# Order on the tensor engine in a KV-cache decode kernel: value sums ahead of a new load's first transposes, and both transposes of the 40-key load ahead of the value sums

## Chip, cores and metric

One core of a Trainium2 chip; later batches of runs were on other chips, so medians are compared within the same rounds. The metric is the device time of one execution in microseconds, from the first to the last instruction and the launch around it; the profile's own span is 1.7 to 2.1 us shorter.

## The reference

One token through a layer-norm, attention over a cache of 32 heads with 32768 keys of 192 numbers each, an output projection, and a small ReLU block. Cut to what matters:

```python
H, Sk, Dh = 32, 32768, 192                      # bf16
scores = einsum("bhqd,bhkd->bhqk", q, k_cache) * Dh ** -0.5
p = softmax(scores); o = einsum("bhqk,bhkd->bhqd", p, v_cache)
h = x + o.reshape(1, 1, H * Dh) @ wo;  out = h + relu(layernorm(h) @ w1) @ w2
```

K and V together are 805 MB, each byte used once.

## The kernel before

Each head is read in four K loads and four V loads of 3072 KB (128 partitions x 64 keys). One load is worked on in two chunks of 32 keys; the last head's last load is cut into 40, 16 and 8 keys per partition, so that little is left to do after the last byte. In each chunk DVE does the dot products of some keys; PE does the rest: it transposes K tiles (`transposes`), ACT copies them out of four PSUM buffers, PE multiplies them with q (`scores_pe`), ACT takes the exponentials (`ep` for PE's keys, `ed` for DVE's), and PE sums the values (`values`). Instructions stand in each engine's queue in the order of the program, and on PE matmuls came out in that order: in the profile before, the last head's value sums of chunk 3, whose inputs were complete at 1884.6 us, start at 1890.16, behind transposes that waited for their load until 1886.77.

```python
def transposes(g, h, c):                        # cut
    if off == 0: g.wait("at", "k", h, ld)       # first chunk of a load: its K has landed
    for k, (b0, nb) in enumerate(tiles(jp)):    # up to 4 tiles, 4 PSUM buffers
        g.wait("cp", *tile_before(h, t))        # ACT has emptied this buffer
        ...

def values(g, h, c):                            # cut
    g.wait("ep", h, c); g.wait("ed", h, c)      # probabilities of this chunk
    ...                                         # 16 matmuls

def pe_head(g, h, turn=None):
    for c in range(NC):                         # NC = 8 chunks
        transposes(g, h, c)
        if c > 0:
            values(g, h, c - 1)
        elif h > 0:
            values(g, h - 1, NC - 1)
            den_mm(g, h - 1)
        scores_pe(g, h, c)
        ...                                     # projection, next head's q

# the SP queue, in the order of its issues (cut):
load(K of load n)
g.wait("PV", hp, 2 * lp + 1)                    # value sums of load n-2's second chunk
load(V of load n)                               # two V buffers
```

So a V buffer is released by the value sums of an odd chunk, and these stood behind the first transposes of the next K load, which wait for that load to land.

The softmax here doesn't subtract the row's maximum and nothing guards it: scores larger than these inputs give would overflow.

## Time and profile before

| | before |
|---|---|
| time, median of the first 3 runs | 1926.88 us (1926.21 to 1927.18) |
| bytes read | 825 MB, 427 to 435 GB/s in every slice of the span but the first (408) and the last (321) |
| PE / DVE / ACT busy | 81% / 80% / 50% |
| PE's wait for a K load at its first transposes | 341.8 us, 127 times |

In the profile's lines, `POOLq L301` is GpSimd's relay, which tells PE that a load has landed.

The page's chain of work that ended last, before (share of the span by engine), says where time is set:

```profile
DMA 76%; PE 22%; SPq 1%; issue 0%; ACT 0%; POOLq 0%; DVE 0%
```

Walked back from the end, almost every step leads to the landing of a K load. In the timeline's lines, the columns are start, duration, engine, line, operation, tiles and count; a bracket gives the idle time before it and what ended it. One more line of the timeline before will be needed, the first transposes of the 40-key load:

```profile
1899.69 1.18 PE L338 MATMUL tp<-ident_f,kt 128*128 128x128 f32 x9
```

The 40-key load had landed at 1898.5.

### The profile page before, as it was taken

What the parts mean: (1) busy time and instruction counts of PE and PEld (TensorE: products, weight loads), DVE (VectorE), ACT (ScalarE), POOL (GpSimd) and SP (SyncE); (2) the same over time, 40 slices, a digit from 0 to 9 for tenths busy, and PEclk for the clock granted to TensorE, in tenths of its full rate; (3) what the DMA queues carried; (4) which work ended last, traced back from release to release, by engine and by line L of the source; (5) the groups of instructions that cost most, each with busy time, mean ns of one, the idle gap of its engine ahead of it and who ended that gap; (6) DMA issues with size and microseconds to landing.
All of it is one profiled execution on the core that took longest, in us unless ns stands there. A gap on an engine that the chain in (4) does not pass through costs nothing.

```text
span 1925.6 us, 36082 instructions
## 1 busy us (share of the span) xinstructions
PE 1563.4 (81%) x15899; PEld 1074.8 (56%) x15899; DVE 1546.3 (80%) x670; ACT 970.6 (50%) x2031; POOL 0.7 (0%) x6
## 2 busy tenths in 40 slices
PE   5887888787887888788788878888778888888788
PEld 4555555555555555555555555555555555555555
DVE  5888888787887888887788878888778887888786
ACT  4554555454554554555454554545445454545554
POOL 0000000000000000000000000000000000000000
PEclk8889888888989898888888888888888888898888
DMA  9999999999999999999999999999999999999997
GB/s 408 430 432 433 433 432 432 433 433 431 433 430 433 433 433 433 433 432 427 434 433 433 433 431 433 430 435 432 430 431 431 435 432 433 431 431 429 431 432 321
DMA packets 44799, 825.31 MB, mean 429 GB/s; under 512 B 4580, under 2 KB 6116, under 8 KB 12132
## 3 DMA queue, kind: packets, MB, share of 16 engines
q1 hardware_dynamic: 44762, 824.99, 99.8%
q8 instruction: 12, 0.20, 0.0%
q14 instruction: 15, 0.12, 0.0%
q10 hardware_dynamic: 10, 0.00, 0.0%
HBM read 824.97 MB, written 0.00 MB: 428 GB/s over the span
## 4 chain that ended last, share of the span: by engine, by line
DMA 76%; PE 22%; SPq 1%; issue 0%; ACT 0%; POOLq 0%; DVE 0%
DMA kt<-in_A_k_cache_dram 76%; PE o_ps L319 11%; PE tp L338 10%; SPq L221 1%; PE mm L319 1%; PE sp L319 0%; PE attT L319 0%; ACT kT L533 0%; POOLq L301 0%; DVE o_pair L631 0%; ACT pB L539 0%; PE mm L522 0%; ACT h1T L595 0%; DVE y_row L699 0%; DVE h_col L681 0%
## 5 line engine op out<-in xcount | busy, mean ns | idle before, releaser
L617 DVE TENSOR_TENSOR pr<-kt,qb 128x2304 f32<-128x2304 bf16 (+2 forms) x257 | 755.8, 2941 | 298.9 <-DMA kt<-in_A_k_cache_dram 282.6
L533 ACT COPY kT<-tp 128x1024 bf16<-128x1024 bf16 (+1 forms) x899 | 818.9, 992 | 342.2 <-PE tp L338 340.2
L338 PE MATMUL tp<-ident_f,kt 128*128 128x128 f32 x3459 | 571.7, 332 | 341.8 <-POOLq L301 341.8
L620 DVE TENSOR_REDUCE sc<-pr 128x12 f32<-128x2304 f32 (+2 forms) x257 | 755.3, 2939 | 8.9
L338 PEld LDWEIGHTS tp<-ident_f,kt 128*128 128x128 f32 x3459 | 498.1, 173 | 358.7 <-POOLq L301 357.5
L319 PE MATMUL o_ps<-vt,pB 128*2 128x384 bf16 x2286 | 470.9, 357 | 3.5 <-POOLq L301 3.4
L319 PE MATMUL o_ps<-vt,pA 128*2 128x384 bf16 x1778 | 331.0, 326 | 0.0
L319 PEld LDWEIGHTS o_ps<-vt,pB 128*2 128x2 bf16 x2286 | 184.1, 89 | 239.8 <-issue 87.6
L539 ACT ACTIVATE pB<-sp 128x20 bf16<-128x20 f32 (+2 forms) x258 | 47.9, 186 | 503.1 <-PE sp L319 503.1
L319 PEld LDWEIGHTS sp<-qm,kT 128*128 128x128 bf16 x6918 | 193.2, 97 | 77.7 <-issue 67.5
L319 PEld LDWEIGHTS o_ps<-vt,pA 128*2 128x2 bf16 x1778 | 151.0, 85 | 144.7 <-issue 8.1
L319 PE MATMUL sp<-qm,kT 128*128 128x2 bf16 x6918 | 212.0, 164 | 3.0 <-ACT kT L533 2.1
L548 ACT ACTIVATE pA<-sc 128x12 bf16<-128x12 f32 (+2 forms) x257 | 53.4, 208 | 89.0 <-DVEq L64 88.3
L539 ACT ACTIVATION_READ_ACCUMULATOR pB<-sp 128x1 f32 x258 | 50.2, 195 | 0.0
L548 ACT ACTIVATION_READ_ACCUMULATOR pA<-sc 128x1 f32 x257 | 48.7, 190 | 0.0
L625 DVE TENSOR_REDUCE rec<-mm 128x1 f32<-128x20 f32 x32 | 5.7, 179 | 51.6 <-PE mm L319 51.1
L319 PE MATMUL mm<-wq_s,xn_ln 128*1 (+1 forms) x160 | 18.7, 248 | 3.6 <-POOLq L301 3.6
L631 DVE TENSOR_SCALAR o_pair<-o_ps,rec 2x384 bf16<-2x384 f32 x32 | 19.4, 605 | 2.8 <-PE o_ps L319 1.7
L319 PE MATMUL attT<-oT,wo_s 128*128 128x1 bf16 x465 | 15.9, 163 | 0.3 <-DVE oT L638 0.3
L319 PEld LDWEIGHTS mm<-dsums,ones_mat 128*128 128x128 f32 x64 | 9.5, 188 | 10.7 <-issue 9.3
L319 PE MATMUL mm<-ones_row,row_e 1*128 1x1 bf16 x384 | 14.0, 159 | 0.0
L319 PEld LDWEIGHTS attT<-oT,wo_s 128*128 128x128 bf16 x465 | 13.8, 95 | 0.3 <-DVE oT L638 0.3
(69 smaller groups left out, 129.1 us busy)
## 6 DMA issues: line engine op xcount, KB each, us to landing
kt<-in_A_k_cache_dram SPq DMA_DIRECT2D x127, 3072.0 KB, 22.5
vt<-in_A_v_cache_dram SPq DMA_DIRECT2D x127, 3072.0 KB, 15.5
wq_s<-in_A_wq_dram SPq DMA_DIRECT2D x4, 1920.0 KB, 21.9
wo_s<-in_A_wo_dram SPq DMA_DIRECT2D x16, 480.0 KB, 16.3
kt<-in_A_k_cache_dram SPq DMA_DIRECT2D x1, 1920.0 KB, 19.7
kt<-in_A_v_cache_dram SPq DMA_DIRECT2D x2, 960.0 KB, 24.3
kt<-in_B_w_dram SPq DMA_DIRECT2D x1, 1920.0 KB, 18.3
wq_s<-in_B_w_dram SPq DMA_DIRECT2D x1, 960.0 KB, 20.3
```

The source lines that it names most:

```text
L221: g.do(lambda: nc.sync.dma_start(out=dst, in_=src), sem, label, by=16)
L319: return lambda: pe.matmul(o, lhsT=w, rhs=r, **kw)
L338: calls.append(lambda b=b, o=o: pe.transpose(out=dst[:, b, :], in_=src[:, o:o + 2 * P].bitcast(f32), identity=ident_f[:]))
L533: g.do(lambda: act.copy(out=kT[c % 2][:, b0:b0 + nb, :], in_=src[:, 0:nb, :].bitcast(bf16)), "act_pe", ("cp", h, c, k))
L539: g.do(lambda: act.activation(out=pB[c % 4][:, 0:jp], in_=sp[:, 0:jp], func=F.Exp, scale=SCALE, accum_out=dsums[:, 2 * c + 1:2 * c + 2]), ...
L548: g.do(lambda: act.activation(out=pA[c % 4][:, 0:jd], in_=sc[c % NC][:, 0:jd], func=F.Exp, scale=SCALE, accum_out=dsums[:, 2 * c:2 * c + 1 ...
L617: g.chain(lambda: dve.tensor_tensor(out=pr[:, 0:j1 - j0, :], in0=src[:, (off + j0) * Dh:(off + j1) * Dh].rearrange("p (j d) -> p j d", d=D ...
L620: g.chain(lambda: dve.reduce_sum(out=sc[c % NC][:, j0:j1], in_=pr[:, 0:j1 - j0, :], axis=X), "dve")
L625: g.chain(lambda: dve.reduce_sum(out=rec[:, 0:1], in_=mm[:, 0:2 * NCM], axis=X), "dve")
L631: g.do(lambda: dve.tensor_scalar_mul(out=o_pair[:, :, h % 2, :], in0=o_ps[0:2, 0:2 * Dh].rearrange("q (i d) -> q i d", i=2), scalar1=rec[0 ...
```

## The change

The intent: PE should not stand before a load that has not landed while value sums are ready; V buffers would come free earlier. At the end, the transposes of both halves of the 40-key load go first, so that ACT gets their copies sooner.

```diff
+    def pe_chunk(g, h, c):
+        if c % 2 == 1:
+            transposes(g, h, c)
+        if c > 0:
+            values(g, h, c - 1)
+        elif h > 0:
+            values(g, h - 1, NC - 1)
+            den_mm(g, h - 1)
+        if c % 2 == 0:
+            transposes(g, h, c)
+        scores_pe(g, h, c)
     def pe_head(g, h, turn=None):
         for c in range(NC):
-            transposes(g, h, c)
-            ...                     # values, den_mm, scores as above
+            pe_chunk(g, h, c)
     # the last head: pe_chunk for chunks 0 to 5 in the same way (cut), then, E0 = 6:
         transposes(g, h, E0)
+        transposes(g, h, E0 + 1)
         values(g, h, E0 - 1)
-        for c in range(E0 + 1, NCM):
-            transposes(g, h, c)
-            scores_pe(g, h, c - 1)
-            if c > E0 + 1:
-                values(g, h, c - 2)
+        scores_pe(g, h, E0)
+        transposes(g, h, E0 + 2)
+        scores_pe(g, h, E0 + 1)
+        values(g, h, E0)
+        ...                         # E0 + 3 in the same way as before
```

More of the change, by code (lines that the diff above doesn't have):

```diff
@@ L442, in q_spread @@
         pe_group(g, calls, ("qs", h), "pe_act")
+    def pe_chunk(g, h, c):
[9 more added lines that the diff above has]
+        scores_pe(g, h, c)
     def pe_head(g, h, turn=None):
         for c in range(NC):
-            transposes(g, h, c)
-            if c > 0:
-                values(g, h, c - 1)
-            elif h > 0:
-                values(g, h - 1, NC - 1)
-                den_mm(g, h - 1)
-            scores_pe(g, h, c)
+            pe_chunk(g, h, c)
             if c == 1 and h > 0:
@@ L482, in pe_end @@
         for c in range(E0):
-            transposes(g, h, c)
-            if c > 0:
-                values(g, h, c - 1)
-            else:
-                values(g, h - 1, NC - 1)
-                den_mm(g, h - 1)
-            scores_pe(g, h, c)
+            pe_chunk(g, h, c)
             if c == 1:
@@ L492, in pe_end @@
         transposes(g, h, E0)
+        transposes(g, h, E0 + 1)
         values(g, h, E0 - 1)
-        for c in range(E0 + 1, NCM):
-            transposes(g, h, c)
-            scores_pe(g, h, c - 1)
-            if c > E0 + 1:
-                values(g, h, c - 2)
+        scores_pe(g, h, E0)
+        transposes(g, h, E0 + 2)
+        scores_pe(g, h, E0 + 1)
+        values(g, h, E0)
+        transposes(g, h, E0 + 3)
+        scores_pe(g, h, E0 + 2)
+        values(g, h, E0 + 1)
         scores_pe(g, h, NCM - 1)
```

## The prediction

> **What bounds the kernel now.** I read the page's DMA rows first, then the waits, the DMA issues, and last the timeline of the final 50 us.
>
> The page, in 40 slices of 48 us, then its traffic:
>
> ```profile
> DMA  9999999999999999999999999999999999999997
> GB/s 408 430 432 433 433 432 432 433 433 431 433 430 433 433 433 433 433 432 427 434 433 433 433 431 433 430 435 432 430 431 431 435 432 433 431 431 429 431 432 321
> HBM read 824.97 MB, written 0.00 MB: 428 GB/s over the span
> ```
>
> The 16 DMA engines are busy in every slice but the last, at about 432 GB/s. 825.3 MB at 432 GB/s is 1910 us, against a span of 1925.6. The rest is about 4 us of start and a tail after the last large transfer. PE (1563 us busy) and DVE (1546) have some 20% to spare; per load of 64 keys (128 of them) that is 12.2 us of PE and 12.1 of DVE, in a period that two transfers of 3072 KB set: 6.29 MB / 432 GB/s = 14.6 us.
>
> The waits (engine, tile, line, releaser: total us, times, longest) and the issues (size, median us to landing):
>
> ```profile
> PE tp L338 <- POOLq L301: 341.8, 127, 7.2
> PE sp L319 <- ACT kT L533: 2.1, 4, 1.3
> ```
>
> ```profile
> kt<-in_A_k_cache_dram SPq DMA_DIRECT2D x127, 3072.0 KB, 22.5
> vt<-in_A_v_cache_dram SPq DMA_DIRECT2D x127, 3072.0 KB, 15.5
> ```
>
> The first line is the wait the change is aimed at: once per K load, PE stands in front of the first transposes of that load, 341.8 / 127 = 2.7 us, although the value sums behind them have their inputs. The value sums then end late, and the V buffer they release is refilled late. But the issue lines say what that lateness costs: V itself needs 3.146 MB / 432 GB/s = 7.3 us, and lands 15.5 us after its issue. So some 8.2 us of earlier transfers are typically still queued when it is issued. The queue does not run dry, and the wait is paid for by DMA time.
>
> The timeline of the end (start, duration):
>
> ```profile
> 1884.39 0.19 ACT L548 ACTIVATION_READ_ACCUMULATOR pA<-sc 128x1 f32 x1
> 1886.77 3.46 PE L338 MATMUL tp<-ident_f,kt 128*128 128x128 f32 x15 [2.79 <-POOLq L301]
> ...
> 1890.16 2.72 PE L319 MATMUL o_ps<-vt,pB 128*2 128x384 bf16 x8
> ...
> 1894.17 0.91 PE L319 MATMUL sp<-qm,kT 128*128 128x2 bf16 x30
> ...
> 1896.38 1.79 PE L319 MATMUL o_ps<-vt,pB 128*2 128x384 bf16 x10
> ```
>
> ```profile
> 1912.48 0.40 PE L319 MATMUL mm<-dsums,ones_mat 128*128 128x20 f32 x2 [0.36 <-ACT pB L539]
> ...
> 1914.96 0.60 DVE L631 TENSOR_SCALAR o_pair<-o_ps,rec 2x384 bf16<-2x384 f32 x1 [1.66 <-PE o_ps L319]
> ...
> 1919.63 1.72 PE L319 MATMUL attT<-h1T,wq_s 128*128 128x1 bf16 x60 [0.36 <-ACT h1T L595]
> ```
>
> From the landing of the last full K load (1886.7) PE is busy nearly without a gap to 1914.9, when the last value sum ends; then a fixed serial finish of 10.7 us follows. Here PE order sets the end, so here alone the change can gain.
>
> [...] (after the 2.8 us gap 15 transposes took 3.46 us, while 12 at full clock take 1.52), so a moved gap also moves a slow stretch.
>
> **The change part by part.** Nothing is added or removed: same instructions, same transfers in the same order.
>
> *Part 1, value sums ahead of even chunks' transposes.* The value sums of an odd chunk (16 matmuls; the same 16 took 2.7 to 2.8 us at full clock from 1896.38 on) move into the 2.7 us gap. In the timeline at 1857.6 they would run at about 1854.7 to 1857.4 instead of 1860.1 to 1863.8; the V issue moves from 1863.9 to about 1857.4, 6.5 us earlier. Queue depth grows from 8.2 to about 14.7 us. DMA time gained: none, because it was never empty. The cost: ACT's four copies of the first chunk (3.55 us, starting about 0.7 us after the transposes) used to be hidden behind those value sums; now PE ends its 15 transposes after about 2.1 us and waits about 0.7 + 3.55 - 2.1 = 2.1 us for the copies. So most of the old wait returns as a wait for ACT. PE then needs about 11 us at full clock plus 2.1, still under 14.6; DVE starts at the K landing as before. Steady state: 0 us.
>
> *The end, up to the 40-key load.* Value sums of chunk 3 run from 1884.6 to 1887.3; transposes to about 1889.5; copies to 1891.55 (before: 1891.47); scores at 1891.65 instead of 1894.17, 2.5 us earlier; ACT's two exponentials to 1893.3; next transposes to about 1894.0; the next V load, issued at 1878.42 with the median 15.5, lands at 1893.9, so value sums 4 take until about 1896.8, and scores 5 until about 1897.6, 2.2 us earlier than the 1899.8 of before. But the 40-key K load was issued at 1878.8 and took 19.7 us: it lands at 1898.5. Its position in the queue does not change, so only 1899.7 - 1898.5 = 1.1 us of the 2.2 is kept.
>
> *Part 2, both transposes of the 40-key load first.* Starting at 1898.55: first transposes 1.2 us; the second must wait for transposed-tile buffers that ACT empties (copies 2.20 us, not before DVE's sums at 1898.7 and their exponential), ending at about 1901.4; value sums 5 to 1904.1; scores 6 to 1904.7; transposes 8 to 1905.5; scores 7 from 1905.55 to 1906.1, no longer held until 1906.6 by ACT's exponential; value sums 6 to 1907.75; transposes 9 to 1908.6; scores 8 to 1909.0; value sums 7 to 1910.7; scores 9 to 1911.1; exponential, and the denominator at 1911.5 instead of 1912.48. Part 2 by itself removes about 0.8 us of one wait on ACT and spends about 0.7 waiting for buffers: near 0. Sum at the denominator: 0.95 us. After it nothing changes, except that the last w2 piece (issued 1908.32, 11.0 us to landing: 1919.3) becomes close: the final 60 matmuls would start at 1918.7 and need it after 50 of them, at 1920.1. It fits.
>
> So 1926.9 - 0.95 = **1925.9 us**, a gain of 0.05%.
>
> **The rivals.**
> *No gain.* The new 2.1 us gap at 1889.5 may drop the clock. Value sums at low clock took 3.7 to 4.0 us against 2.7; that would end scores 5 at about 1899 to 1900 and eat the 1.1 us: 1926.9. For it: gaps of 2.3 us in this profile were followed by slow transposes. Against it: there is 0.9 us of slack before the 40-key load.
> *PE or ACT becomes the bound.* If the exposed copies cost more than 2.1 us and the clock stays low, PE's 12.2 + 2.1 = 14.3 us comes near the 14.6 period. A few us at most, since 12.2 already includes slow stretches and queue depth is larger: 1927 to 1930. Unlikely.
> *A deeper queue lifts the DMA rate.* Slices of 427 to 430 could rise to 433; all at 433 would be worth about 4 us: 1922. Against it: at every V issue the trace has earlier transfers still to land, the last of them 6.95 us later or more, so those dips are not an empty queue. Unlikely.
> *Earlier w1 and w2.* They are issued after value sums 3, so about 7 us earlier; but they stand behind the same bytes, and the finish did not wait for them: nothing.
>
> **Range and chances.** Three runs of before spread by 1.0 us. The gain is between 0 (clock) and about 2 us (40-key load a little early, clock high): 1924.4 to 1927.3 for 8 in 10. Two per cent is 38 us, several times the whole tail after the last landing, and the DMA floor alone is 1914. Faster by over 2%: 0.005; slower by over 2%: 0.01; within: 0.985.
>
> **What would show each step.** Right: DMA slices unchanged near 432; the transposes' wait for POOL falls from 341.8 to under 130 us, while scores wait for ACT's copies 150 to 280 us (before 2.1); V's median to landing rises from 15.5 to about 22, K's from 22.5 to about 29; the first transposes of the 40-key load start at its landing, about 1898.5; the denominator comes about 1 us earlier. Wrong: if the mean rate changes by more than 1 GB/s, if V's time to landing stays near 15.5, or if the transposes of the 40-key load still start over 0.5 us after it has landed.

## The result

The changed kernel took 1927.9 us (median of 4, 1927.51 to 1929.7) against 1926.99 (1926.21 to 1927.18) in the same rounds. The ratio is 1.0007, with a 95% interval of 0.999 to 1.0025. (A ratio here is the mean time of one kernel's runs over that of the other's of the same rounds, so not quite the ratio of the medians.) The interval holds 1, so by itself it proves no loss. But the predicted gain of 0.95 us did not come, and 1927.9 lies above the predicted range.

All chips together, the kernel before ran 40 times, median 1926.6 us, 12 runs above 1927; the changed one ran 17 times, median 1927.8, with 16 above 1927 and a highest of 1929.96. The spread is the first clue: an added fixed cost alone would shift the runs, not stretch them.

After, the page's chain, the two large issues, and two lines of the waits:

```profile
PE 46%; DMA 26%; ACT 16%; DVE 10%; issue 1%; SPq 0%; DVEq 0%; ACTq 0%; POOLq 0%
...
kt<-in_A_k_cache_dram SPq DMA_DIRECT2D x127, 3072.0 KB, 27.0
vt<-in_A_v_cache_dram SPq DMA_DIRECT2D x127, 3072.0 KB, 20.0
```

```profile
PE sp L319 <- ACT kT L537: 306.2, 127, 2.4
...
PE tp L338 <- POOLq L301: 12.7, 4, 5.2
```

The removed wait is gone (341.8 to 12.7 us), and another has replaced it almost whole: scores now wait 2.4 us per load for ACT's copies (2.1 to 306.2 us in all). V lands 20 us after its issue in place of 15.5, so it is issued about 4.5 us earlier, and that bought nothing: the mean rate over the span is 429 GB/s in both kernels, and the 40-key load lands at 1898.5 in both. The new thing is the chain: it no longer jumps from landing to landing but runs through PE and ACT for long stretches.

The end of the changed kernel in that profiled run, PE's lines of the timeline:

```profile
1884.60 1.46 PE L319 MATMUL o_ps<-vt,pB 128*2 128x384 bf16 x8 [0.74 <-ACT pA L552]
...
1887.29 1.86 PE L338 MATMUL tp<-ident_f,kt 128*128 128x128 f32 x15
...
1891.58 0.96 PE L319 MATMUL sp<-qm,kT 128*128 128x2 bf16 x30 [2.44 <-ACT kT L537]
...
1892.40 2.80 PE L338 MATMUL tp<-ident_f,kt 128*128 128x128 f32 x12
...
1895.13 3.20 PE L319 MATMUL o_ps<-vt,pB 128*2 128x384 bf16 x10
...
1899.86 2.40 PE L338 MATMUL tp<-ident_f,kt 128*128 128x128 f32 x17
...
1912.47 0.40 PE L319 MATMUL mm<-dsums,ones_mat 128*128 128x20 f32 x2 [0.36 <-ACT pB L543]
```

The first three lines are on the predicted times (1884.6, 1887.3, 1891.65). Then the 12 transposes take 2.80 us in place of 1.5 and the value sums behind them last to 1899.3 in place of 1896.8. The 40-key load's transposes start at 1899.86, not at the landing, and the denominator is at 1912.47, where it was before (1912.48).

The clock shows why. Windows of 6 us, before and after; the columns are busy time and count for PE, PE's weight loads, DVE, ACT and POOL, then the granted clock, DMA share and GB/s:

```profile
1886.70:1892.70 6.00, 5.93 (x24) 4.05 (x25) 5.82 (x3) 3.55 (x4) 0.00 (x0) 0.50 0.96 408
```

```profile
1892.00:1898.00 6.00, 6.00 (x43) 3.92 (x41) 5.96 (x2) 3.31 (x7) 0.00 (x0) 0.50 0.99 413
```

Both windows lie wholly at half clock (0.50). By the clock records of the traces the stretch is 6.83 us long in both, from 1886.05 before and from 1891.22 after. Before, it follows PE's wait for the K load; after, it follows the wait for ACT's copies, 5.2 us later. It was moved, not removed.

### The profile page after: what moved, and what is told of

It reads as the page before. It is cut to its first block, busy times and chain, and to the rows that moved or that the text cites. A ratio compares the mean times of both kernels' runs of the same rounds, so it can differ in the third digit from the quotient of the medians.

```text
span 1925.7 us, 36082 instructions
## 1 busy us (share of the span) xinstructions
PE 1525.6 (79%) x15899; PEld 1032.5 (54%) x15899; DVE 1546.5 (80%) x670; ACT 966.2 (50%) x2031; POOL 0.7 (0%) x6
## 4 chain that ended last, share of the span: by engine, by line
PE 46%; DMA 26%; ACT 16%; DVE 10%; issue 1%; SPq 0%; DVEq 0%; ACTq 0%; POOLq 0%
PE o_ps L319 26%; DMA kt<-in_A_k_cache_dram 26%; ACT kT L537 14%; PE tp L338 11%; PE sp L319 7%; DVE sc L624 5%; DVE pr L621 5%; ACT pA L552 1%; PE mm L319 1%; ACT pB L543 1%; PE attT L319 1%; SPq L221 0%; DVE o_pair L635 0%; DVE rec L629 0%; DVE rec L630 0%
## 5 line engine op out<-in xcount | busy, mean ns | idle before, releaser
L338 PE MATMUL tp<-ident_f,kt 128*128 128x128 f32 x3459 | 524.3, 313 | 13.2 <-POOLq L301 12.7
L338 PEld LDWEIGHTS tp<-ident_f,kt 128*128 128x128 f32 x3459 | 455.5, 162 | 46.3 <-issue 30.5
L319 PE MATMUL sp<-qm,kT 128*128 128x2 bf16 x6918 | 214.7, 164 | 306.2 <-ACT kT L537 306.2
L552 ACT ACTIVATE pA<-sc 128x12 bf16<-128x12 f32 (+2 forms) x257 | 52.7, 205 | 15.5 <-DVEq L64 15.4
L319 PEld LDWEIGHTS mm<-ones_row,row_e 1*128 1x128 bf16 x384 | 15.6, 99 | 0.3
```

What stands on the lines that cost most here:

```text
L319: return lambda: pe.matmul(o, lhsT=w, rhs=r, **kw)
L338: calls.append(lambda b=b, o=o: pe.transpose(out=dst[:, b, :], in_=src[:, o:o + 2 * P].bitcast(f32), identity=ident_f[:]))
L552: g.do(lambda: act.activation(out=pA[c % 4][:, 0:jd], in_=sc[c % NC][:, 0:jd], func=F.Exp, scale=SCALE, accum_out=dsums[:, 2 * c:2 * c + 1 ...
```

## The experiments

The theories. **Clock:** the gap before scores 4 of the last head is followed by a slow stretch that eats the gain. **Queue:** the deeper DMA queue costs something in the steady part. A third, **carried lateness**, came up on the way. Each kernel ran in five rounds unless it is called a look. Every kernel gave a correct result. Every ratio's interval holds 1, so the medians and spreads below are read together with the profiles, which show the mechanism by themselves.

| run | this, us (lowest to highest) | before, same rounds |
|---|---|---|
| a0, changed again | 1928.07 (1925.97 to 1929.0) | 1926.47 |
| e1, part 1 alone | 1927.87 (1926.24 to 1929.06) | 1926.47 |
| e2, part 2 alone | 1926.40 (1926.06 to 1926.85) | 1926.47 |
| e3, changed, gap filled | 1926.23 (1926.06 to 1927.36) | 1926.47 |
| e4, pair of transposes, last head | 1926.26 (1926.03 to 1926.54) | 1926.25 |
| e5, changed, old order at chunk 4 | 1926.14 (1926.0 to 1926.3) | 1926.25 |
| e6, before, new order at chunk 4 | 1927.18 (1926.59 to 1927.77) | 1926.25 |
| e8, before, gap filled | 1926.39 (1926.24 to 1926.63) | 1926.25 |
| a1, a2, a3, looks at the changed one | 1929.24, 1927.68, 1927.70 | 1926.91 |
| e9, changed, gap half filled | 1926.67 (1926.46 to 1927.93) | 1926.91 |
| a4, changed again | 1927.84 (1927.41 to 1929.96) | 1926.73 |
| e11, changed, old order at chunk 2 | 1926.58 (1926.15 to 1927.98) | 1926.73 |
| e10, pair of transposes, every load | 1926.43 (1926.26 to 1926.59) | 1926.73 |

**The change again (a0), no edit.**

> The changed kernel once more, timed in five rounds, to see whether the 0.9 us between the medians (1927.9 against 1927.0) is real. Theory A (the DMA queue sets the time, the tail's gain was eaten by a slow clock after the new gap, so nothing changed): ratio 1.0000 within 0.0004, that is within 0.8 us. Theory B (the earlier V issues, that is the deeper DMA queue, cost something in the steady part): 0.5 to 1.5 us slower, with the mean DMA rate or the landing of the 40-key load later by as much.

The difference of medians was 1.6 us, twice what the clock theory allowed (0.8), with the same wide spread. By luck its profiled run was its fastest, 1925.97 us, and in it the slow stretch is missing: the granted clock was 1.00 in every window from 1880 to 1904. PE's timeline:

```profile
1892.17 1.51 PE L338 MATMUL tp<-ident_f,kt 128*128 128x128 f32 x12
1893.82 1.79 PE L319 MATMUL o_ps<-vt,pB 128*2 128x384 bf16 x10
...
1898.33 2.42 PE L338 MATMUL tp<-ident_f,kt 128*128 128x128 f32 x17 [1.06 <-DMA kt<-in_A_k_cache_dram]
```

Here every step up to the 40-key load is as the prediction had it; PE even waits 1.06 us for that load. The predicted time (1925.9) exists, in a minority of executions: one of the 17 runs was below 1927. Against the median of the kernel before in the same rounds that is a gain of 0.5 us, not 0.95.

**Part 1 alone (e1)**: the end's last block put back to the old order.

```diff
-        transposes(g, h, E0 + 1)    # and the unrolled block behind it
+        for c in range(E0 + 1, NCM): ...   # as before
```

> Part 1 alone: value sums ahead of the even chunks' transposes, the end in its old order. Theory A: the first transposes of the 40-key load again start near 1899.8 (clock low after the gap of about 2.4 us before the scores of chunk 4), the denominator at 1912.2 to 1912.6, the time within 0.5 us of the kernel before. Theory B: slower by the same 0.5 to 1.5 us as the whole change, since the V issues are the same.

It behaves like the whole change (1927.87), with chunk 5's transposes at 2.80 us and the 40-key load's at 1899.88. Both theories had room for that: the profile went as the clock theory said, the time by more than its 0.5 us.

**Part 2 alone (e2)**: the kernel before with only the end's last block changed.

> Part 2 alone: only the order of the end. V issues as before (V 15.5 us to landing). My prediction's sum has part 2 at about 0: the denominator within 0.3 us of 1912.5 and the time within 0.5 us of the kernel before. Theory B says exactly that as well, so here a loss of 0.5 us or more would speak against B.

As expected: no change. From the 40-key load's first transposes to the denominator it is 12.62 us here (1899.25 to 1911.87), against 12.79 before: part 2 is worth some 0.2 us, inside the noise of the timing.

**The gap filled with idle matmuls (e3)**: the changed kernel and, at one place of the last head, 18 matmuls whose result nobody reads.

```diff
+    def fill(g, n):
+        for _ in range(n):
+            g.do(mmul(mm[:, 256:512], ident_b[:], ident_f[:].bitcast(bf16), start=True, stop=True))
             transposes(g, h, c)        # chunk 4 of the last head
+            fill(g, 18)            # simplified: as an argument of pe_chunk
         scores_pe(g, h, c)
```

> The whole change, plus 18 idle matmuls (a constant times a constant into unused PSUM columns, the result is not read) in the last head between the transposes and the scores of chunk 4, some 2 us in the gap of 2.4. Theory A: the clock stays high, the 12 transposes of chunk 5 take about 1.5 us in place of 2.8 and the value sums of chunk 4 about 2.8 in place of 4.2, so scores 5 end near 1897.6, the first transposes of the 40-key load start at its landing near 1898.5 instead of 1899.86, and denominator and end come 0.8 to 1.2 us earlier than in the changed kernel. Rival (the tail is held by DVE or ACT, not by PE): transposes of the 40-key load earlier, but the denominator still at 1912.3 or later.

PE's timeline of that run:

```profile
1890.33 2.13 PE L319 MATMUL mm<-ident_f,ident_b 128*128 128x256 bf16 x18
1892.93 0.90 PE L319 MATMUL sp<-qm,kT 128*128 128x2 bf16 x30 [0.47 <-ACT kT L542]
1893.69 1.51 PE L338 MATMUL tp<-ident_f,kt 128*128 128x128 f32 x12
...
1898.44 2.39 PE L338 MATMUL tp<-ident_f,kt 128*128 128x128 f32 x17
...
1911.06 0.40 PE L319 MATMUL mm<-dsums,ones_mat 128*128 128x20 f32 x2 [0.36 <-ACT pB L548]
```

Useless work in one gap of 2.4 us, in one of 32 heads, took 1.8 us off the median of the same rounds (1928.07 to 1926.23). The steady part, with its early V issues, is untouched. PE was even 2.2 us late at the last full load in this profile, and still started the 40-key load's transposes 0.2 us after its landing (1898.26). The 12 transposes behind the gap took 1.51 us in place of 2.80, as long as in a0, where the granted clock was 1.00. So the clock in this place matters, and the rival that DVE or ACT holds the tail falls: the denominator moved with PE.

**Both transposes together in the last head (e4)**: chunk 5's transposes are real work for the same gap.

```diff
-            pe_chunk(g, h, 4); pe_chunk(g, h, 5)     # simplified
+        values(g, h, 3); transposes(g, h, 4); transposes(g, h, 5)
+        scores_pe(g, h, 4); values(g, h, 4); scores_pe(g, h, 5)
```

> The whole change, and in the last head the gap is filled with real work: both transposes of the last full K load together (chunk 5's right behind chunk 4's), then scores 4, value sums 4, scores 5. Clock theory (the loss of the changed kernel, 1928.0 against 1926.5, comes from the slow clock after the gap ahead of scores 4, in the last head only): chunk 5's transposes fall into the gap, value sums 4 wait for their V until about 1893.9 and run at full clock, the 40-key load's transposes start near 1898.4, the denominator near 1911.0; median 1926.0 to 1926.6, about 1.5 us under the changed kernel. Rival (short gaps, of which this order has several, slow the clock as well): 1927 to 1928.

1926.26, nothing above 1926.54, 40-key transposes at 1898.47, as the clock theory had it. Gaps of 0.26 to 0.70 us did no harm in this profile: the value sums and scores behind them are as short as in a0 (1.14 us for the last 6 value sums of chunk 4, 0.75 for scores 5).

**Old order at chunk 4 of the last head only (e5)**, all else changed.

> The whole change except for one place: chunk 4 of the last head keeps its old order (transposes, then value sums). All earlier V issues are as early as in the changed kernel. Clock theory: as the kernel before with the new end, 1926.2 to 1926.8, no loss; V still lands about 20 us after its issue. Rival (the deeper queue of the steady part costs the 1.5 us): 1927.5 to 1928.5, as the changed kernel.

1926.14, the lowest median of all, with V still 20.2 us from issue to landing. The queue theory is refuted: the same deep queue, no loss.

**New order at chunk 4 of the last head only (e6)**, all else as before.

> The kernel before with the new order at one place alone: chunk 4 of the last head. Clock theory: the whole loss is here, median 1927.5 to 1928.5 and a wide spread (1926 to 1929.5), with slow transposes of chunk 5 (2.8 us) in the slow ones. Rival (steady part): 1926.2 to 1926.8, as before.

```profile
1892.32 2.80 PE L338 MATMUL tp<-ident_f,kt 128*128 128x128 f32 x12
1895.05 1.97 PE L319 MATMUL o_ps<-vt,pB 128*2 128x384 bf16 x10
...
1898.54 1.18 PE L338 MATMUL tp<-ident_f,kt 128*128 128x128 f32 x9
```

Only half a hit. One moved call in the whole kernel gives slow transposes and a loss of 0.9 us. But the median is below the expected range, and nothing came near 1929: the slowest executions are not explained here. The run profiled was the fastest (1926.59); its slow stretch was 3.41 us long, not 6.83 (granted clock 0.57 from 1892 to 1896), and its 40-key transposes still start 0.1 us after the landing. The slower ones, up to 1927.77, were not profiled.

**The kernel before with its own gap filled (e8).**

```diff
+            if c == E0 - 2: fill(g, 18)     # ahead of chunk 4's transposes, last head
             transposes(g, h, c)
```

> The kernel before, its order untouched, with 18 idle matmuls (2.1 us) in the last head's wait for the last full K load. If the clock is what the tail's time turns on, and not the order: its transposes after that wait take about 1.9 us in place of 3.46, the value sums after them 2.8 in place of 4.0, the 40-key load's transposes start at its landing near 1898.4, and the time falls by 0.5 to 1.2 us below the kernel before, to about 1925.6. If the order is what counts: within 0.3 us of the kernel before.

```profile
1884.96 2.12 PE L319 MATMUL mm<-ident_f,ident_b 128*128 128x256 bf16 x18
1886.92 1.80 PE L338 MATMUL tp<-ident_f,kt 128*128 128x128 f32 x15
...
1898.40 1.20 PE L338 MATMUL tp<-ident_f,kt 128*128 128x128 f32 x9 [1.08 <-DMA kt<-in_A_k_cache_dram]
```

The mechanism came as expected (1.80 us for 15 transposes in place of 3.46, and PE waiting for the 40-key load), the time did not fall: the kernel before ran at 1926.25 in these rounds. That is the floor: once PE is ready when the 40-key load lands, nothing PE does earlier counts. The run of before that was profiled first, 1927.44 us, was one of its slower ones; my expectation took it for the typical one.

**Three looks at the changed kernel (a1, a2, a3), no edit**, to catch a slow execution.

> The changed kernel unaltered, one look with a profile, to catch one of its slow executions (up to 1929.7). Clock theory: the span follows the start of the 40-key load's transposes, that is the later scores 5 end the later the denominator, microsecond for microsecond, and the DMA landings do not move: a run of 1929 us would show those transposes near 1901 to 1902 with the value sums of chunk 4 wholly at the low clock; a run of 1926 would show them at the landing, near 1898.4. Rival: a slow run shows the 40-key load landing later by the difference.

> As the look before it: another execution of the same kernel, judged in the same way.

> As the two looks before it: another execution of the same kernel, judged in the same way.

The first look was the catch, 1929.24 us:

```profile
1886.19 1.46 PE L319 MATMUL o_ps<-vt,pB 128*2 128x384 bf16 x8 [0.56 <-ACT pA L552]
...
1894.00 2.80 PE L338 MATMUL tp<-ident_f,kt 128*128 128x128 f32 x12
1896.73 3.29 PE L319 MATMUL o_ps<-vt,pB 128*2 128x384 bf16 x10
...
1901.54 2.39 PE L338 MATMUL tp<-ident_f,kt 128*128 128x128 f32 x17
```

Its 40-key load landed at 1898.77, 0.3 us later than in the others, so the DMA is not the cause; the transposes start 2.8 us after it. The local slow stretch is the same as ever (2.80 and 3.29 us). What is new is the first line: PE reached the value sums of chunk 3 at 1886.19 in place of 1884.60, already 1.6 us late.

Over all profiles of the changed kernel, the profile's span is the start of the 40-key load's transposes plus a constant, worked out from the traces:

| run | transposes of the 40-key load | span | difference |
|---|---|---|---|
| a0 | 1898.33 | 1924.2 | 25.9 |
| first profile | 1899.86 | 1925.7 | 25.8 |
| a2 | 1899.93 | 1925.8 | 25.9 |
| a3 | 1900.05 | 1925.9 | 25.9 |
| a1 | 1901.54 | 1927.4 | 25.9 |
| a4 | 1902.32 | 1928.2 | 25.9 |

So the whole spread of 4 us is decided before that instruction starts.

**Why one execution keeps its clock.** The kept traces say more than the runs were made for. Each records when the granted clock changed, between 1.00 and 0.50. In the profile before (214 stretches) and the first profile of the change (156) every stretch begins a whole number of steps of 3.413 us after the first one, to within 1 ns. Those at half clock last one step (73 and 52 times), two (30 and 23) or three (3 and 2), leaving out the last one, which ends with the trace. All 17 traces show this grid, to within 2 ns; where it stands against the loads differs from execution to execution. The step is a measured length of these traces, and they do not show what makes it. The first profile of the change, then a0, by steps of their own grids:

```profile
1887.80:1891.22 3.42, 1.34 (x13) 1.10 (x11) 3.39 (x2) 3.24 (x4) 0.00 (x0) 1.00 0.96 410
1891.22:1898.04 6.82, 6.46 (x52) 4.39 (x53) 6.64 (x3) 3.62 (x8) 0.00 (x0) 0.50 0.99 412
```

```profile
1887.05:1890.46 3.41, 1.92 (x16) 1.62 (x15) 3.38 (x2) 2.65 (x3) 0.00 (x0) 1.00 0.93 395
1890.46:1893.87 3.41, 2.33 (x43) 2.09 (x44) 3.26 (x2) 2.38 (x8) 0.00 (x0) 1.00 0.98 411
```

In the first, one step holds most of the 2.44 us gap (PE is busy for 1.34 us of the step's 3.42), and the next two steps, 6.82 us, run at half clock. In a0 two steps share the gap, and the clock stays full. The same gap stands before the scores of nearly every load: 124 times in the first profile of the changed kernel, 745 times in all six. Where one step held 2.0 us of it or more, half clock followed in 59 of 59 cases of the first profile and in 341 of 344 of all six; elsewhere in 8 of 65 and in 87 of 401. This is read from traces of one program; no run shifted the grid on purpose, and the 87 show that the gap's place is not all that counts.

**The gap half filled (e9)**: 9 idle matmuls, 1.45 us of idle time left.

> The changed kernel with 9 idle matmuls in the gap of chunk 4 of the last head in place of 18, so some 1.4 us of the gap of 2.4 stay idle. If gaps of about 1.4 us leave the clock alone (the pair order had gaps of under 1 us and lost nothing): 1926.0 to 1926.6, as with 18. If a gap of that length still lowers the clock in part of the executions: a median between 1926.6 and 1928 and a wider spread.

1926.67, with two of five runs at 1927.56 and 1927.93. In the profiled run (1926.53) the slow stretch is missing: the 12 transposes behind the gap took 1.51 us. The median fits the second branch and the spread points to it; no slow run of it was profiled, so that gaps of this length lower the clock is likely, not shown.

**The change in the same rounds as the next two (a4).** These three were run because the lateness of a1 was still unexplained.

> The changed kernel in the same rounds as the two variants after it: median 1927.4 to 1928.4, spread up to 1929.7; PE starts the first transposes of a K load a median of some 1.8 us after its landing, by up to 5 us or so.

1927.84, as expected; the profiled run, 1929.96, was again a slow one. The lateness of the first transposes of a K load after its landing, worked out from the trace's records over the 127 loads: median 2.4 us, up to 6.2. In the first profile of the changed kernel it was 1.9 and 6.4; before, 0.09 and 0.10.

**Old order at chunk 2 of the last head (e11)**: PE is made to meet one K landing shortly before the end.

> The whole change, but chunk 2 of the last head in the old order (transposes as soon as the K load lands, then the value sums). If lateness is carried from load to load: PE is back at the landing there, arrives at chunk 4 on time in every execution, and only the local slow clock is left: median 1926.6 to 1927.6 and nothing above 1928.3, as in the run with the new order at chunk 4 alone (1927.2). If nothing is carried: as the changed kernel, with runs near 1929.

1926.58, 1.3 us below the changed kernel of the same rounds, with the local gap of 2.44 us still there. Its median is a hair under the expected range and its highest, 1927.98, is inside it. It shows less about carried lateness than its median suggests. In its profile PE starts the last full load's transposes 0.65 us after the landing, but so it does in the first profile, a2 and a3 of the changed kernel (0.65 to 0.71 us). Those start the 40-key load's transposes 1.4 to 1.5 us after the landing, this one 0.25 us:

```profile
1892.43 1.80 PE L338 MATMUL tp<-ident_f,kt 128*128 128x128 f32 x12
...
1898.81 2.40 PE L338 MATMUL tp<-ident_f,kt 128*128 128x128 f32 x17
```

The difference is the slow stretch: one step of 3.41 us here (granted clock 0.72 from 1892 to 1898), two steps there (0.50 over the same 6 us of the first profile). So lateness is not what makes the usual loss. It does separate the slowest executions: a1 and a4 were 1.95 and 3.10 us late at the last full load, and 2.8 and 3.9 us at the 40-key load. That e11 has no run above 1928 fits this; five runs do not prove it.

**Both transposes together in every load (e10).**

```diff
+    def pe_pair(g, h, c):
+        if c % 2 == 0:
+            ...values(c - 1)
+            transposes(g, h, c); transposes(g, h, c + 1)
+        else:
+            values(g, h, c - 1)
+        scores_pe(g, h, c)
```

> The change with both chunks' transposes together in every K load: value sums of the load before, both transposes, scores, value sums, scores. The second transposes run in the gap where the first ones wait for the copies, so PE needs some 1.5 us less per load than in the changed kernel. If the lack of slack per period is what carries lateness: the waits of scores for copies fall from 306 us to under 220, the lateness of the first transposes falls below a median of 1.5 us, and the time is at its floor, 1926.0 to 1926.6, with no run over 1927. Rival (short gaps slow the clock anyway, or the transposes' buffers stall PE as long): 1927 or more.

1926.43, nothing above 1926.59: the time is as expected, and so is the wait of scores for copies (no longer among the long ones; 46.3 us on the weight loads). The lateness is not: its median is still 1.6 us, against under 1.5 expected. In the profiled run PE is 2.9 us late at the last full load:

```profile
1889.50 2.41 PE L338 MATMUL tp<-ident_f,kt 128*128 128x128 f32 x19
...
1898.66 2.39 PE L338 MATMUL tp<-ident_f,kt 128*128 128x128 f32 x17
```

Still, the 40-key load's transposes start 0.3 us after its landing (1898.39). From the one to the other PE takes 9.2 us here, 12.6 in the first profile of the change and 9.8 in e3 with its idle matmuls: most of what is saved is the clock, full from 1884.57 on by the trace's clock records (from 1886.81 on each set of 8 value sums takes 1.46 us, against 2.72 at 1870.91), and 0.6 us is the shorter way. Nor does this order spare the clock everywhere: the mean granted clock over the span is 0.891, against 0.906 in the first profile of the change. So e10 shows that the end is saved when its gap is filled; it does not show that lateness disappears.

No version beats both kernels by more than the noise: e2, e3, e4, e5, e8 and e10 all sit at 1926.1 to 1926.4, the floor that the landing of the 40-key load sets; they only avoid the slower runs.

## Why the prediction was wrong

**Right:** the DMA engines stayed busy, and earlier V issues gained nothing (rate 429 GB/s in both). **Right:** the wait turns into a wait for copies (predicted 150 to 280 us, measured 306). **Right:** part 2 is near 0 (0.2 us). **A size off:** V's time to landing rose to 20.0, not 22, and K's to 27.0, not 29; PE's own median lateness of 1.9 us fits the missing 2.

**Wrong, the main step:** "next transposes to about 1894.0; ... value sums 4 take until about 1896.8, and scores 5 until about 1897.6". These two terms were put in at full clock, 1.5 and 2.8 us; they measured 2.8 and 4.2, so 2.7 us were missing, and the 40-key load's transposes started 1.4 us after the landing, past the 0.5 us that the prediction had named as a sign of being wrong. The gain of 2.2 us at scores 5 was in fact only the slow clock of the profile before, taken out of the sum for the changed kernel without a reason: without the slow stretch, the old order is through with scores 5 at 1897.3 too (e8, where 15 transposes took 1.80 us and 12 took 1.51; a0, at a granted clock of 1.00, the same). The prediction had seen that "a moved gap also moves a slow stretch", listed it as the rival "no gain", and did not let it into the sum. When the stretch is absent (a0) or prevented (e3), the sum holds.

This step alone makes the loss of a usual execution: the first profile, a2 and a3 (1927.5 to 1927.7 us) were only 0.65 to 0.71 us late at the last full load. a0 was as late there (0.65 us), kept its clock and lost nothing.

**Wrong, a second step, in the slowest executions:** "Steady state: 0 us." Its number was good: 11 plus 2.1 us of PE per load. In the slow look (a1), value sums to value sums take 1886.19 - 1872.99 = 13.2 us with nothing slow in between (15 transposes 1.86 us, 12 transposes 1.51). But 13.2 against a period of 14.55 (two transfers, 6.29 MB, at 432 GB/s) leaves 1.35 us to catch up, and one slow stretch of 6.83 us costs 2.7. In the old order PE stopped at every landing, and every load began on time (0.09 us late); its work from there to scores 5 was 10.4 us in e8, so it had 4 us to spare. In the new order PE is late for loads on end (a median of 1.9 us in the first profile, 2.4 in a4); that it carries slow stretches on from load to load is the author's reading. In the middle this costs nothing that shows in the mean rate. At the end it arrives at the 40-key load, and there it adds to the local stretch: a1 and a4, 1.3 and 2.4 us later than the first profile at the last full load, were 1.4 and 2.5 us later than it at the 40-key load. e6, which has the local stretch without carried lateness, reaches 1927.77 and no higher. The rival "PE or ACT becomes the bound" named this region, 1927 to 1930, and was called unlikely, because "queue depth is larger"; depth kept the DMA's rate (429 GB/s in both), not the end.

**Range:** its upper end, 1927.3, stood on "before" plus noise, with no room for a loss. What stays open is how often the grid of clock steps falls which way, since no run set it, and what besides the gap's place in a step brings the clock down.

## What to carry to other kernels

When you sum instruction times around a moved gap, use the slow times that the profile shows for what follows the new gap (here 2.80 us for 12 transposes, not 1.5), or find other work for the gap; here moving the second transposes into it did that (e4, 1926.26 us). Removing a wait from an engine that is not the bound can also remove the spot where it falls back into step: look at the slack per period after the change (here 1.35 us, where it had been 4), and at what reaches the end. Several profiles of one kernel, above all of a slow run, told more than another median.
